# A gated attention and long-convolution kernel: spectrum and conv rows loaded by GpSimd's queue, four small loads by ScalarE's, and both order strings replaced

## The chip, the cores and the metric

The kernel runs on one core of a Trainium2 chip. Its time is the device time of one execution in microseconds (us). TensorE (PE) does the matmuls, VectorE (DVE) and ScalarE (ACT) the elementwise work, GpSimd (POOL) and SyncE (SP) mostly issue DMAs; ScalarE can issue them as well. [...]

## The reference

Eight batches of 3136 rows. First a gated attention with a squared relu in place of a softmax, then a gated long convolution over the sequence, done with a Fourier transform, and an output projection:

```python
# u, v: (8, 3136, 256); z: (8, 3136, 64)
scores = (1 / 3136) * z @ z.transpose(0, 2, 1)
x = u * (np.maximum(scores, 0.0) ** 2 @ v)
proj = x @ w_proj                       # (8, 3136, 768)
x1, x2, x3 = proj[..., :256], proj[..., 256:512], proj[..., 512:]
X2 = np.fft.rfft(x2, n=3136, axis=1)
H = np.fft.rfft(filter_fft, n=3136, axis=0)[None]
x2_conv = np.fft.irfft(X2 * H, n=3136, axis=1)
out = (x1 * x2_conv * x3) @ w_out       # float32
```

## The kernel before, in words

**Tiles.** The sequence of a batch is cut into seven chunks (five of 512 columns, one of 256, one of 320) and 25 tiles of 128 rows. A score block is `ps_s <- zT_t`; its relu goes to `R_t`, its square to `A_t`, and `ps_o_t <- A_t,v_t` adds it up. The scores are symmetric, so some blocks aren't computed again: SyncE transposes an `A_t` by DMA into `M_t`, `M2e_t` or `M2o_t` (line 1848), and TensorE uses these in a later chunk.

**After a chunk.** VectorE multiplies the sum with `uT_t` into `xT_t`. Projections of `xT_t` give the gates (`gate_t`) and `x_t`. `dft1` multiplies `x_t` with a 64-point transform, the result is evicted to `s_t`, and SyncE puts it into a DRAM scratch, `spec` (line 1007).

**After a batch.** 3136 = 64 x 49. `add_spectrum` loads rows of the scratch in the other order, four loads of 16 frequencies' rows each into `spec_in_t` (two buffers), multiplies with 49-point transforms `S`, then with the filter's spectrum `H` on VectorE, transforms back (`xh` with `TZ`) and puts `gs_t` into a second scratch (line 1358). `load_spec` (line 1037) issues three DMAs for each load; it waits for the puts of the batch's chunks, for a free buffer, and for the load before it. `add_end` loads that second scratch chunk by chunk into `conv_in_t` (two buffers, `load_c`, line 1064), transforms (`T`), multiplies with the gates into `yT_t`, projects with `wo` and stores `ost_t` to `out_dram` (line 1467). This work is spread over the next batch's attention as filling work. The filter's own spectrum goes through `load_spec` as well, once.

**The last batch** has nothing behind it. There `load_parts` (line 1052) splits each of the four spectrum loads: a first piece of the transforms' rows that are there early, and a small second piece of 9 rows (two DMAs each) that waits for the last puts. The first two loads go to `spec_in_t`, the other two to `gs_t`. The last conv loads go to `A_t` and `v_t`.

**GpSimd** issues the loads of u, v and z that cast to bf16 (`cast_u`, `load_rows`, `cast_rows`), each group behind a `tick`, a small copy that waits for a chunk's `xT_t` (line 643). u and z are then transposed by DMA from SyncE (lines 1521, 1575).

**What sets the order.** All work is first described as tasks. `Plan.go` plays them through with costs and due times of its own and emits them in the order that results. Two strings, found by a search outside the kernel, make its choices: each letter of `ORDER` says which queue TensorE takes its next task from (S scores, Q quads of the spectrum, W sums over v, w and v such a sum in two row halves, A and B projections, transforms and ends, Z the same late in the last batch), and each letter of `ENGINES` gives one free eviction or square to ScalarE or VectorE. S, Q, w and v run in 64-row parts of the array, the others over 128 rows. SyncE and GpSimd get their DMAs in the order in which the plan finds them ready. `LATE_...` values are allowances that the plan adds to a DMA's landing; `MOST` says how many single PSUM banks it may hold at once.

Of the kernel before, what the change touches and what calls it, by code (L numbers as in the profile page):

```python
# [38 lines left out]
MOST = 3  # L39
# [7 lines left out]
    "ASSAWSSSWWAAWSwvwSvSSwvwSSvWSSSWBWWSSWWWWWSSSWWWWWAwwSSSvWvSSSWWWWWAWWWAWBASBWWWWAASwSwSvwvSSBWAAWAW"  # L47
    "SSSvWWWAWABWAWABWAWWBBAWWSSSWWSSWWSSSWAAWWWSSSWWAWBWABWAAWWWWSSwwSSvBWBAWSvSSWWWWWWAWWWAASSWWABWWAWB"
    "WAASwSSvSWBAWAAWSSWWBWWAAWWAWWSSwSWAAAWSwSSWAAWvSSvSWWAWWWWAWSSAWWAAWWSSSWAWWWAASSwQvwSSAAWASvQSWWWW"
    "AWAWWSQSWWWAAAWSwQSvwSwQSvvwSQSWWWAASSvAWWWWAAWSSQWWWWSSAAWAWQwSSvwSwSQvvwSvSQWWAWWWSQQWWAAAWWWWSwSQ"  # L50
    "WWAAAWQSSwSWvSSvWAWAWWAAWQQSWAWAWWQSSWWAWWSQSWAASSWWAAWQQQWWAWWWSQWWAAWSSWAAWAWWWwSwQSvSvWWSQSWWWSSA"
    "WAWWWWSwSSwwSvSSvvWWAAAWWWSSSWWWWAAWAWAWWWSSwSvSBBAWWBBAWSSAAWSwSSWABBWAWASSvWWABBWWBWSSWWWBABWABAWS"
    "SSWAAWWSSSWBWASSBWAWWWBAWWWBAAWWBAAWBWSSAAWSSABWAAWSSSWWBBAWSQQWWWWWBWQSAWWWWSwSwwQvQvSvSWABWBASQAWB"
    "WQSQWAWAAWBWWSSQWWAAWWSSWAWSSQWAWSQQWSwwQSvvSAWWAWWAWWWSQQWWAWAWWSSSWWWBWAAAQSWAWWWSSSWWWSSAWAWWSSSW"
    "AAWSwSvSWWAWWAWWWAWWSSSWWWWBWSSSWAAWBBWSAAWSSSWWBBWBWSSBBWBAWWAWWBAWWASSWABAWSwSSWABAWBSSBAWBWSSvSWW"
    "BBWWWAABWAAWWSSSWWAWAWQSAABWWQSSWWWBAWSSAWAWBAWQSSWWWWSQSWWABWWAWQSQWWQSQWWBASSWWAAAWWQSAWWAWSQBAWWA"
    "WSSSWWBWSQQWWQSSWWAWWSSSWWWAWWQSWWAWWWAAWASwSAWWSSvQWAWWQSSWWAAWWSSAWAAAWAWSSSWBAAWWSSSWWWBSSWAWWWWW"
    "BWBBWWBAWASSwwSSWAAWBAWSSSvvwSABWBABWBASvSWBWBWWBWAAWWBWSSSWWBAAWAABSSWBwSSSWWBWBAWSvSSWABAWWAWWSSWA"
    "BWWABWSSSWBWSQAAWWAASSWWQQSWAWAWWBAAQQWWBWWBSSWWWWSSQWWWSQSWAAAWSSSWWAAWWWQQSWWBWAAWAWWQSSwQWSQWWSQS"
    "WWWAWWQQvSWAWWAWAWAWWWWAASSWWAWSSSWWQSAAWWWSSSWWAAWAAWAWSSWWAwSwSSvvwSvSWWWAWWAWWWSSBWWBWASSWAAWSSSW"  # L60
    "ABWWBSSAWAWBWASAWBAAWBWWBWAWSSSWWBBSSWWAWBWABASwSvSSWBABWBWSSSWWWABWBWWWSSWBWWWSSSWWAAWSSSWWSQSWAAWA"
    "SSAWAWABWAWABWAWAWWBWAWQQwSSWvSSQWWBWQQSWAWAWWAWSQSWWWWQSQWWBAWSSBWWSSQWWAWWSwSQvSWWABWAWWWAQSWBAWWA"
    "ASQWAWWQSAAWWSSSWWAAWAWWWSSSWWWAWwSSwQvvQSSWWAAWSSWWABWBWWWWWAAWSSSWWWAAWSSSWABWWSSSWABWBAWABBSSWAWA"
    "WWBBAWAWBSSWBBWAWBSSAWAWBASSWAAWSSSWBBBWAWSSSWBWAAWWSSWBBWWAAWAWAWAWSSSWWWAWSwQSvwQSvWWWABWAAAWWWQQS"
    "WWWAASSWBAWSSWBWBAAASSWSQQWWWSSQWWBWBAWWAWWQSSWAWBWAAAWQQQWWSSQWWWSQSWAWAAWWQQSWWAWAWSSWWWAWAAWQWAWS"
    "SSWWAWWSSABAWWSSSWWWWwSSSWWABAWWvSSSWWAAWSSWBWAWWWBWAWASSWBBAWWSSSWAASSWABWWBAWSSSWWWBSSBBWWWAWAWBWB"
    "AWBABWSSWBBAWWSSSWBBWSwSSvSWWWWBBAWWBBWWSSQWWBSSQWWWBAWWSQSWWSSSWAAWWWWWQQWWSSWWAAWWSSQWWQSSWWAAWWAA"
    "WSSQWWWBWWQSSWAWAWWSQQWWQSSWWWSSSWWAWAWWWWWQSSWWWWBAAWWQQSWABAWSSWAWWQSBWWWSSSWWWWWAWWSSSWWWWZWWWWWW"
    "ZAZAZZAAZBAZBZZBZBBZBZZBZBQQZZZQQQQQZZBBQQQQQQQBQQZZZBZZZZBZZZBZBZZZBZZZZZZBBBBBBBBBBBBBBBBBBBBBBBBB"
# [146 lines left out]
class Task:  # L216


    def __init__(self, emit, cost, deps=(), takes=(), prio=0, lat=None, moves=0.0, late=0.0):
        self.emit, self.cost, self.takes, self.prio = emit, cost, list(takes), prio  # L220
        self.lat, self.moves, self.late = lat, moves, late
        self.deps = [d if isinstance(d, tuple) else (d, None) for d in deps]
        self.kids, self.frees = [], []
        self.left = len(self.deps)
        self.ready = 0.0
        self.end = None
        self.holders = 1
        self.ports = ()
        self.second, self.split, self.flips, self.flip = None, False, False, None
        for d, _ in self.deps:  # L230
            d.kids.append(self)
# [9 lines left out]
class Plan:  # L241


    def __init__(self):
# [11 lines left out]
        self.bus = 0.0  # L256
        self.port = {"DVE": 0.0, "POOL": 0.0}
# [32 lines left out]
    def run(self, task, engine, start):  # L290
# [4 lines left out]
        if engine == "PE" and start < SLOW_TO:  # L295
            cost *= 2
        end = start + cost
# [133 lines left out]
def kernel(  # L431
# [599 lines left out]
    def load_spec(src, j0, nj, deps, late=0.0, home=l_p):  # L1031
        box = {}

        def go():
            box["t"] = home.tile([P, 8, D], BF16)
            for rows, part in by_row(src, box["t"], 2 * j0, 2 * nj):
                nc.sync.dma_start(out=part, in_=rows)

        t = on("SP", go, 1.5, [*deps, *((d, ISSUED) for d in loads[-1:])], [home.slots], moves=0.345 * nj, late=late)
# [4 lines left out]
    def load_parts(src, j0, nj, first, rest, home):  # L1044
        box = {}

        def go(lo, hi):
# [3 lines left out]
            for r in range(2):  # L1051
                nc.sync.dma_start(out=box["t"][r * N1 + lo : r * N1 + hi, 0 : 2 * nj, :], in_=rows[r])

        a = on("SP", lambda: go(0, LATE_Q), 1.0, first, [home.slots], moves=0.29 * nj, late=1.0)
        return a, on("SP", lambda: go(LATE_Q, N2), 1.0, [*first, *rest, (a, ISSUED)], prio=-1, moves=0.06 * nj, late=0.5), box

    def load_c(src, c, deps, home):
# [3 lines left out]
        def go():  # L1061
            box["t"] = home.tile([P, 4, D], BF16)
            view = src[ds(t0 * P, nt * P), :].rearrange("(t p) d -> p t d", t=nt)
            nc.sync.dma_start(out=box["t"][:, 0:nt, :], in_=view)
# [3 lines left out]
        return on("SP", go, 0.55, deps, [home.slots], moves=0.235 * nt, late=1.7), box  # L1068
# [113 lines left out]
    def add_proj(b, c, xt, xt_tasks):  # L1182
# [49 lines left out]
        def to_spectrum():  # L1232
            t0, n = T0[c], len(tiles[c])
            at = 0
            while at < n:
# [13 lines left out]
                def ev2(e, nt=nt, box=box):  # L1249
# [9 lines left out]
                        [e2, t1_done], (a, 1), late=LATE_PUT * (b < B - 1),  # L1259
# [248 lines left out]
    plan.bus = 17.5  # L1508
# [8 lines left out]
    def load_uT(b, c, deps):  # L1517
# [9 lines left out]
        if isinstance(made, tuple):  # L1527
            t = after(on("SP", go, 1.3, deps, [uT_p.slots], moves=0.385 * u_tiles(c), late=LATE_TURN), made[1])
            t.frees.append((Held(un_p.slots, made[0]), 0))
        else:  # L1530
            t = on("SP", go, 1.3, [*deps, made], [uT_p.slots], moves=0.385 * u_tiles(c), late=LATE_TURN)
            t.frees.append((made, 0))
        u_tasks[b, c] = t
# [17 lines left out]
    def casts_at(b, c):  # L1551
# [3 lines left out]
        if n < B and 0 <= i < 4:  # L1555
            t0, t1 = ((0, 8), (8, 16), (16, 22), (22, NT))[i]

            def go_z(tick_):
# [26 lines left out]
                t = on("SP", turn, 1.3, [d, *z_tasks.get(n, [])[-1:]], [zT_p.slots] if first else [], moves=0.196 * (t1 - t0), late=LATE_TURN)  # L1585
                t.frees.append((d, 0))
# [233 lines left out]
    def mirror(un, q_):  # L1820
# [13 lines left out]
        for a, i, ts in runs:  # L1834
# [18 lines left out]
            )  # L1853
            made.append(t_)
# [212 lines left out]
```

## Time and profile before

| | |
|---|---|
| runs | 971.87 us median of 3 (966.74 to 972.98) |
| profiled execution | 974.7 us, span 972.9 us, granted TensorE clock 0.992 |
| TensorE busy | 939.0 us (97%) |
| VectorE, ScalarE busy | 862.1 us (89%), 839.6 us (86%) |
| GpSimd busy | 198.0 us (20%) |
| DMA moved | 170.36 MB, 64.6% of the DMA engines' span by SyncE's queue, 23.8% by GpSimd's |

A row of a stretch has its start and end, its length, and for TensorE, its weight loads, VectorE, ScalarE and GpSimd the busy time with the count of instructions, then the granted TensorE clock, the DMA engines' busy share and GB/s. A row of the chain has start, length and what it was; the chain is followed back from the last instruction to what released each step. `SPq` and `ACTq` are instructions of an engine's sequencer, DMA issues above all. A row of a line has a count, then shortest, median and longest duration in ns, first and last start.

### The profile page before, as it was taken

How to read it: one execution, taken by the hardware profiler on the slowest of the kernel's cores; microseconds unless marked ns; L12 is line 12 of the kernel's file. 1: busy time of each engine (PE TensorE's matmuls, PEld its weight loads, DVE VectorE, ACT ScalarE, POOL GpSimd, SP SyncE). 2: the span in 40 equal slices, each digit the busy share in tenths (PEclk: the TensorE clock that was granted, in tenths of full speed). 3: DMA queues.
4: the chain of work that ended last, by engine and by line, in shares of the span. 5: the costliest groups of instructions: out<-in, count | busy, mean ns of one | idle time of the engine just before them, and what ended most of it. 6: DMA issues, size and time to landing. Idle time of an engine off the chain costs nothing.

```text
span 972.9 us, 20144 instructions
## 1 busy us (share of the span) xinstructions
PE 939.0 (97%) x7077; PEld 478.1 (49%) x7180; DVE 862.1 (89%) x1499; ACT 839.6 (86%) x1154; POOL 198.0 (20%) x426
## 2 busy tenths in 40 slices
PE   8999999999999999999999999899999999999986
PEld 3344544455444654445544555345554455544644
DVE  8997989998699998999889987689989999998786
ACT  7887899999899889988888998799897999899873
POOL 5223212220311221122111221121212211001031
PEclk9999999999999999999999999999999999999998
DMA  9998989967999889978899798987799968996768
GB/s 154 167 193 162 158 151 180 181 131 138 182 220 196 147 171 191 220 151 161 180 199 191 132 169 160 199 176 144 160 192 212 196 140 174 186 202 109 206 172 252
DMA packets 332406, 170.36 MB, mean 175 GB/s; under 512 B 242598, under 2 KB 307942, under 8 KB 332304
## 3 DMA queue, kind: packets, MB, share of 16 engines
q1 hardware_dynamic: 302496, 132.43, 64.6%
q0 software_dynamic: 29168, 35.13, 23.8%
q10 hardware_dynamic: 640, 1.51, 0.5%
q8 instruction: 56, 0.92, 0.4%
q14 instruction: 46, 0.38, 0.1%
HBM read 90.26 MB, written 53.35 MB: 148 GB/s over the span
## 4 chain that ended last, share of the span: by engine, by line
PE 87%; DMA 5%; DVE 2%; issue 2%; ACT 1%; SPq 1%; DVEq 0%; ACTq 0%
PE ps_o_t L560 46%; PE ps_s L560 35%; PE ps_o_t L1719 6%; DMA M_t<-spec_in_t 1%; DMA M2o_t<-A_t 1%; DMA spec_in_t<-spec 1%; DMA conv_in_t<-spec 1%; DMA ost_t<-in_z_dram 1%; ACT R_t L1918 1%; DVE gate_t L1218 1%; DMA gs_t<-spec 1%; DMA spec<-s_t 0%; SPq L670 0%; DVE x_t L597 0%; DVE yT_t L1407 0%
## 5 line engine op out<-in xcount | busy, mean ns | idle before, releaser
L560 PE MATMUL ps_o_t<-A_t,v_t 128*128 128x512 bf16 (+2 forms) x1768 | 409.8, 355 | 7.1 <-issue 4.6
L1918 ACT ACTIVATE R_t<-ps_s 128x1024 f32<-128x1024 f32 (+3 forms) x347 | 320.8, 957 | 42.9 <-PE ps_s L560 38.9
L560 PEld LDWEIGHTS <-v_t 128*128 128x128 bf16 x2462 | 222.9, 98 | 227.1 <-issue 62.1
L1927 ACT ACTIVATE A_t<-R_t 128x1024 bf16<-128x1024 f32 (+3 forms) x321 | 312.2, 1000 | 7.3 <-DVE R_t L1920 2.7
L1920 DVE TENSOR_SCALAR R_t<-ps_s 128x1024 f32<-128x1024 f32 (+4 forms) x165 | 185.6, 1135 | 27.4 <-PE ps_s L560 20.2
L1929 DVE TENSOR_TENSOR A_t<-R_t 128x1024 bf16<-128x1024 f32 (+2 forms) x171 | 187.7, 1108 | 12.2 <-ACT R_t L1918 11.5
L560 PE MATMUL ps_s<-zT_t 64*128 64x512 bf16 (+5 forms) x1381 | 163.6, 356 | 1.2 <-DVE zT_t L597 0.5
L643 POOL COPY tick<-xT_t 1x1 bf16<-1x1 bf16 x54 | 11.6, 214 | 666.3 <-DVE xT_t L1973 666.3
L560 PE MATMUL ps_s<-xT_t,wp 128*128 128x512 bf16 (+2 forms) x407 | 107.9, 352 | 0.8 <-issue 0.3
L593 ACT ACTIVATE x_t<-ps_s 128x512 bf16<-128x512 f32 (+2 forms) x144 | 80.8, 570 | 30.6 <-PE ps_s L560 26.9
L560 PEld LDWEIGHTS <-zT_t 64*128 64x128 bf16 (+1 forms) x1414 | 53.5, 99 | 83.9 <-issue 63.2
L1310 DVE TENSOR_TENSOR xh<-xh,H 128x1024 bf16<-128x1024 bf16 x120 | 82.0, 685 | 2.9 <-ACT xh L593 1.5
L1973 DVE SCALAR_TENSOR_TENSOR xT_t<-ps_o_t,uT_t 128x256 bf16<-128x256 f32 (+2 forms) x224 | 76.1, 382 | 7.7 <-PE ps_o_t L560 5.9
L1218 DVE TENSOR_TENSOR gate_t<-ps_s,x_t 128x256 bf16<-128x256 f32 (+2 forms) x210 | 71.4, 384 | 10.8 <-PE ps_s L560 8.3
L560 PE MATMUL ps_o_t<-M_t,v_t 128*128 128x512 bf16 (+2 forms) x316 | 71.9, 350 | 0.9 <-DMA M_t<-spec_in_t 0.7
L1407 DVE TENSOR_TENSOR yT_t<-ps_s,gate_t 128x512 bf16<-128x512 f32 (+2 forms) x97 | 58.6, 617 | 9.2 <-PE ps_s L560 6.5
L593 ACT ACTIVATE s_t<-ps_s 128x512 bf16<-128x512 f32 (+1 forms) x83 | 48.5, 590 | 15.8 <-PE ps_s L560 15.0
L634 POOL DMA_DIRECT2D un_t<-in_u_dram x112 | 59.8, 556 | 6.8 <-issue 3.4
L560 PEld LDWEIGHTS <-wp 128*128 128x128 bf16 x448 | 41.6, 98 | 39.2 <-issue 7.6
L653 POOL DMA_DIRECT2D v_t<-in_v_dram x112 | 59.0, 547 | 9.2 <-issue 7.4
L560 PE MATMUL ps_s<-wp,xT_t 128*128 128x256 bf16 x396 | 58.9, 274 | 0.1
L560 PE MATMUL ps_s<-wo,yT_t 128*128 128x256 bf16 (+1 forms) x342 | 52.1, 275 | 0.2
(175 smaller groups left out, 995.2 us busy)
## 6 DMA issues: line engine op xcount, KB each, us to landing
out_dram<-ost_t SPq DMA_DIRECT2D x60, 256.0 KB
spec<-s_t SPq DMA_DIRECT2D x96, 128.0 KB
spec_in_t<-spec SPq DMA_DIRECT2D x56, 192.0 KB
spec<-gs_t SPq DMA_DIRECT2D x56, 192.0 KB
v_t<-in_v_dram POOLq DMA_DIRECT2D x80, 128.0 KB, 4.7
un_t<-in_u_dram POOLq DMA_DIRECT2D x80, 128.0 KB, 5.3
conv_in_t<-spec SPq DMA_DIRECT2D x34, 256.0 KB
out_dram<-ost_t SPq DMA_DIRECT2D x18, 128.0 KB
```

The costliest lines, as they stand in the source:

```text
L560: wrote(nc.tensor.matmul(o, *args, **kw), o)
L593: got = nc.scalar.activation(out_, in_, AF.Copy)
L634: nc.gpsimd.dma_start(out=t[ds(j * N1, N1), lo - t0 : hi - t0, :], in_=x[:, n2 : n2 + hi - lo, :])
L653: nc.gpsimd.dma_start(out=t[ds(j * N1, N1), ds(v_at(a), (b - a) * D)], in_=r[:, n2 + a - lo : n2 + b - lo, :].rearrange("p t d -> p (t d)"),)
L1218: got = nc.vector.tensor_tensor(g[:, ::-1] if h == 0 else g, p, x, ALU.mult)
L1310: nc.vector.tensor_tensor(x[:, 1 - i], x[:, 0], h, ALU.mult)
L1407: got = nc.vector.tensor_tensor(yb["y"][:, dh, 0:w], p, gates[b, c, dh][:, 0:w], ALU.mult)
L1918: has_read(nc.scalar.activation(r, p, AF.Relu), p)
L1920: has_read(nc.vector.tensor_single_scalar(r, p, 0.0, ALU.max), p)
L1927: nc.scalar.activation(a, r, AF.Square)
L1929: (nc.vector if e == "DVE" else nc.gpsimd).tensor_tensor(a, r, r, ALU.mult)
L1973: nc.vector.scalar_tensor_tensor(x, f, inv_s2, ut, ALU.mult, ALU.mult)
```

## The change

- `load_spec` issues on GpSimd's queue in place of SyncE's, and so does `load_c` where it fills `conv_in_t`.
- In `load_parts` the small second pieces for `gs_t` go to ScalarE's queue; those for `spec_in_t` and all first pieces stay on SyncE's.
- The plan gets new allowances, and a term `CLOGS`: a transposing DMA costs it more while loads from GpSimd or an earlier transpose are still under way. `MOST` goes from 3 to 6.
- `ORDER` and `ENGINES` are other strings of the same lengths and, for `ORDER`, the same count of each letter. `ENGINES` has 15 letters more for VectorE.

The strings are left out:

```diff
-LATE_PUT, LATE_LOAD, LATE_TURN, LATE_C, LATE_D2 = 1.0, 1.8, 1.0, 1.0, 1.6
-LATE_CAST = 1.5
-LATE_Z = 4.0
+LATE_PUT, LATE_LOAD, LATE_TURN, LATE_C, LATE_D2 = 1.0, 1.8, 0.7, 1.0, 0.5
+LATE_CAST = 1.3
+LATE_Z = 2.2
+CLOGS = ((0.0, 0.0, 0.2, 0.3), (0.0, 0.1, 0.7, 1.2))
-LATE_F = 6.0
+LATE_F = 2.0
-MOST = 3
+MOST = 6
...
+        if task.clogs:
+            cost += CLOGS[self.turned_to > start][min(sum(x > start for x in self.casts), 3)]
...
+            if engine == "POOL":
+                self.casts = [*self.casts[-3:], self.bus]
+            elif task.clogs:
+                self.turned_to = self.bus
...
             for rows, part in by_row(src, box["t"], 2 * j0, 2 * nj):
-                nc.sync.dma_start(out=part, in_=rows)
+                nc.gpsimd.dma_start(out=part, in_=rows)
-        t = on("SP", go, 1.5, [*deps, *((d, ISSUED) for d in loads[-1:])], [home.slots], moves=0.345 * nj, late=late)
+        t = on("POOL", go, 1.6, [*deps, *((d, ISSUED) for d in loads[-1:])], [home.slots], moves=0.345 * nj, late=late)
...
-        def go(lo, hi):
+        def go(lo, hi, by=nc.sync):
...
-                nc.sync.dma_start(out=box["t"][r * N1 + lo : r * N1 + hi, 0 : 2 * nj, :], in_=rows[r])
+                by.dma_start(out=box["t"][r * N1 + lo : r * N1 + hi, 0 : 2 * nj, :], in_=rows[r])
-        a = on("SP", lambda: go(0, LATE_Q), 1.0, first, [home.slots], moves=0.29 * nj, late=1.0)
-        return a, on("SP", lambda: go(LATE_Q, N2), 1.0, [*first, *rest, (a, ISSUED)], prio=-1, moves=0.06 * nj, late=0.5), box
+        a = on("SP", lambda: go(0, LATE_Q), 1.0, first, [home.slots], moves=0.29 * nj, late=1.5 if home is l_p else 2.6)
+        if home is gs_p:
+            return a, on("ACT", lambda: go(LATE_Q, N2, nc.scalar), 1.1, [*first, *rest, (a, ISSUED)], prio=-1, moves=0.06 * nj, late=2.0), box
+        return a, on("SP", lambda: go(LATE_Q, N2), 1.0, [*first, *rest, (a, ISSUED)], prio=-1, moves=0.06 * nj, late=1.5 if home is l_p else 2.6), box
...
-            nc.sync.dma_start(out=box["t"][:, 0:nt, :], in_=view)
+            (nc.gpsimd if home is c_p else nc.sync).dma_start(out=box["t"][:, 0:nt, :], in_=view)
         if home is c_p:
-            return in_order(on("SP", go, 0.55, [*deps, *((d, ISSUED) for d in loads[-1:])], [home.slots], moves=0.235 * nt, late=LATE_C)), box
+            return in_order(on("POOL", go, 0.6, [*deps, *((d, ISSUED) for d in loads[-1:])], [home.slots], moves=0.235 * nt, late=LATE_C)), box
...
-    plan.bus = 17.5
+    plan.bus = 21.0
```

In the built order 142 loads have gone from SyncE to GpSimd (96 for spectra, 46 of conv rows) and four small ones to ScalarE; all other DMAs have kept their engine.

More of the change, by code (lines that the diff above doesn't have):

```diff
@@ L256, in __init__ @@
         self.bus = 0.0
+        self.casts, self.turned_to = [], 0.0
         self.port = {"DVE": 0.0, "POOL": 0.0}
@@ L1063, in go @@
             view = src[ds(t0 * P, nt * P), :].rearrange("(t p) d -> p t d", t=nt)
[L1064 removed]
+            (nc.gpsimd if home is c_p else nc.sync).dma_start(out=box["t"][:, 0:nt, :], in_=view)
         if home is c_p:
[L1067 to L1068 removed]
+            return in_order(on("POOL", go, 0.6, [*deps, *((d, ISSUED) for d in loads[-1:])], [home.slots], moves=0.235 * nt, late=LATE_C)), box
+        return on("SP", go, 0.55, deps, [home.slots], moves=0.235 * nt, late=0.2 if home is A_p else 2.6), box
     def sides(x):
@@ L1258, in to_spectrum @@
                         "FA", lambda box=box, nt=nt: box["x"][:, 0 : nt * D], t0 + at, nt, D1[b % 2],
-                        [e2, t1_done], (a, 1), late=LATE_PUT * (b < B - 1),
+                        [e2, t1_done], (a, 1), late=LATE_PUT if b < B - 1 else (0.2 if c < NC - 2 else 1.7),
                     )
@@ L1527, in load_uT @@
         if isinstance(made, tuple):
-            t = after(on("SP", go, 1.3, deps, [uT_p.slots], moves=0.385 * u_tiles(c), late=LATE_TURN), made[1])
+            t = after(on("SP", go, 1.3, deps, [uT_p.slots], moves=0.385 * u_tiles(c), late=1.0), made[1])
             t.frees.append((Held(un_p.slots, made[0]), 0))
         else:
-            t = on("SP", go, 1.3, [*deps, made], [uT_p.slots], moves=0.385 * u_tiles(c), late=LATE_TURN)
+            t = on("SP", go, 1.3, [*deps, made], [uT_p.slots], moves=0.385 * u_tiles(c), late=1.0)
             t.frees.append((made, 0))
+        t.clogs = True
         u_tasks[b, c] = t
```

85 lines of the change are left out of this document (44 added, 41 removed).

## The prediction

> **What bounds the kernel now.** I read the page first (busy shares, slices), then the busy time in stretches of 25 us, then the chain of waits in order of time, then fine stretches and the timelines of TensorE, SyncE and GpSimd where TensorE pauses.
>
> ```profile
> span 972.9 us, 20144 instructions
> PE 939.0 (97%) x7077; PEld 478.1 (49%) x7180; DVE 862.1 (89%) x1499; ACT 839.6 (86%) x1154; POOL 198.0 (20%) x426
> 800.00:825.00 25.00, 24.89 (x181) 13.21 (x183) 23.29 (x40) 22.87 (x31) 5.02 (x11) 1.00 0.82 168
> 500.00:525.00 25.00, 22.91 (x161) 10.60 (x162) 22.35 (x40) 19.61 (x28) 2.58 (x6) 1.00 1.10 204
> 600.00:625.00 25.00, 21.58 (x141) 9.66 (x139) 18.67 (x26) 20.98 (x24) 3.80 (x8) 1.00 1.12 195
> 625.00:650.00 25.00, 24.73 (x166) 11.60 (x166) 20.00 (x39) 20.80 (x28) 3.81 (x8) 0.93 0.86 174
> 925.00:950.00 25.00, 20.26 (x237) 11.24 (x236) 21.09 (x38) 16.95 (x33) 8.66 (x17) 0.93 0.64 178
> ```
>
> TensorE (first pair of figures after the length) is busy in nearly all of an ordinary stretch, 24.89 of 25 us. So the time is TensorE's own work plus a few pauses. Apart from the start and the end, two stretches stand out, 500 to 525 and 600 to 625, and the second is followed by a lower granted clock (0.93). The chain says what ended those pauses, and the fine stretches size them:
>
> ```profile
> 498.26 9.81 DMA M2o_t<-A_t
> 506.00:510.20 4.20, 2.38 (x16) 0.85 (x17) 2.91 (x7) 1.97 (x2) 0.00 (x0) 1.00 1.12 287
> 613.72 1.27 SPq L1037
> 615.03 9.42 DMA spec_in_t<-spec
> 620.00:624.00 4.00, 1.39 (x10) 0.35 (x8) 2.19 (x2) 2.39 (x3) 0.00 (x0) 1.00 1.34 219
> 624.00:628.00 4.00, 3.35 (x19) 1.78 (x20) 2.95 (x5) 1.53 (x3) 0.00 (x0) 0.74 0.84 179
> 628.00:632.00 4.00, 4.00 (x18) 1.35 (x16) 1.51 (x4) 2.39 (x5) 0.00 (x0) 0.83 0.93 199
> 920.38 4.11 DMA spec<-s_t
> 926.71 5.20 DMA gs_t<-spec
> 924.00:928.00 4.00, 2.55 (x31) 1.59 (x29) 2.33 (x6) 1.88 (x4) 2.11 (x4) 1.00 0.60 169
> 928.00:932.00 4.00, 2.02 (x22) 0.96 (x24) 4.00 (x8) 3.65 (x8) 0.00 (x0) 1.00 0.73 240
> 932.00:936.00 4.00, 4.00 (x46) 3.00 (x50) 1.80 (x4) 3.16 (x7) 0.00 (x0) 0.64 0.03 8
> 936.00:940.00 4.00, 3.79 (x62) 1.90 (x59) 4.00 (x8) 3.54 (x8) 3.18 (x6) 0.93 0.63 139
> ```
>
> Three pauses follow. **At 506**, 4.20 - 2.38 = 1.8 us: an `A_t` buffer is free only when a transposing DMA of 9.81 us has read it. **At 620**, (4.00 - 1.39) + (4.00 - 3.35) = 3.3 us: a spectrum load of 9.42 us is late; then the clock falls to 0.74 and 0.83 for two stretches, (0.26 + 0.17) x 4 = 1.7 us of work; 5.0 us in all. **At 924**, 1.45 + 1.98 = 3.4 us: the last batch's spectrum waits for its last put (4.11 us), then its small second pieces (5.20 us); the clock then takes (0.36 + 0.07) x 4 = 1.7 us. Together 11.9 us; more than these, the start and the loose end no move of a queue can win.
>
> **The change part by part.**
>
> *Spectrum and conv loads leave SyncE for GpSimd.*
>
> ```profile
> L1037 SPq DMA_DIRECT2D spec_in_t<-spec x84: 302/513/1942, 144.6 to 871.0; - x84
> L1064 SPq DMA_DIRECT2D conv_in_t<-spec x46: 359/497/1355, 215.2 to 928.7; - x46
> L653 POOL DMA_DIRECT2D v_t<-in_v_dram x112: 509/547/667, 2.5 to 802.5; - x112
> POOL tick L643 <- DVE xT_t L1973: 666.3, 54, 21.4
> DMA to landing us min/median/max: 4.9/5.6/7.0
> 613.72 4.25 SPq L1037 DMA_DIRECT2D spec_in_t<-spec  x6
> 613.42 1.08 POOL L653 DMA_DIRECT2D v_t<-in_v_dram  x2
> ```
>
> 84 + 46 issues, and 12 more for the filter's spectrum by the built order, leave SyncE, 142 of about 0.5 us each (some 71 us); on GpSimd each costs 0.55 us, 78 us. GpSimd sits 666 us waiting in its `tick` copies, so the issue time itself costs nothing; without that cover it would be the 78 us. What can cost is the order: GpSimd now waits for the last put of a batch, and behind that wait stand a `tick` and the u, v and z casts of the next chunk. A tick waits 666.3 / 54 = 12.3 us on average, more than the 4.11 us of a put, so I take nothing for it; the other bound is a rival below.
>
> No load of these rows from GpSimd is in the trace. Its nearest landings are the filter loads of 256 KB, 4.9 to 7.0 us (the sixth row), against 9.42 us for the late load on SyncE. At 613.7 that load needed 4.25 us for six issues while GpSimd sent v rows from 613.4 on, so it ran beside them. In the changed order the six issues and those casts are in one queue, loads of the next spectra ahead of that chunk's casts, and SyncE's transposes no longer stand behind loads. Bounds for the two middle pauses, 1.8 + 5.0 = 6.8 us: all of it gone, or all of it kept (the transfers share the same engines: the DMA share is over 1 in those stretches; and the new search also lowers the planner's allowances for late transfers). Between them I take the middle, **-3.4 us**, since the larger pause is the moved load's own and the smaller is a transpose's.
>
> Here a rule speaks against the change: the Trainium skill, DMA: Bandwidth & Descriptors, section "Issuing engines are not separate DMA queues", says that DMAs started from several engines share the same 16 DMA engines and that spreading them saves only issue time. By that rule this term would be 0 and the time that of the second rival. Another, SBUF — State Buffer, section "SBUF: two separate sides", says that VectorE in a two-port mode keeps GpSimd from writing DMA descriptors. In this trace GpSimd's issues take 509 to 667 ns beside a VectorE that is 89% busy, so such waits, if there are any, are small; the sum has no term for them.
>
> *The last spectrum's small pieces go to ScalarE.*
>
> ```profile
> 924.62 1.69 SPq L1052 DMA_DIRECT2D spec_in_t<-spec  x4
> 926.35 2.21 SPq L1052 DMA_DIRECT2D gs_t<-spec  x4
> L1467 ACTq DMA_DIRECT2D out_dram<-gs_t x2: 517/560/604, 961.6 to 965.2; - x2
> L1467 ACTq DMA_DIRECT2D out_dram<-xh x2: 795/1074/1353, 964.2 to 966.3; - x2
> ```
>
> SyncE issued eight pieces in a row; the first pair for `gs_t` was out only at some 927.4. With ScalarE issuing four beside it, the pair is out after two issues of 0.52 to 1.35 us, between 925.7 and 927.3: 0.1 to 1.7 us sooner; I take 1.3 (nearer to the shorter issues). ScalarE holds still until the put lands, with evictions behind it; they are of work that TensorE has done already, and ScalarE had 0.4 to 0.5 us gaps there anyway.
>
> The order of TensorE ahead of that wait changes too. Behind the last `x_t,T` matmul the kernel before has 6 pairs of `xT_t,wp`, 4 fours of `wo` and 5 fours of conv work ahead of the spectrum; the changed one 8, 6 and 8.
>
> ```profile
> 922.98 0.60 PE L560 MATMUL ps_s<-wo,yT_t 128*128 128x256 bf16 x4
> 923.42 0.59 PE L560 MATMUL ps_s<-xT_t,wp 128*128 128x512 bf16 x2
> 923.85 0.39 PE L560 MATMUL ps_o_t<-T,v_t 128*128 128x128 bf16 x4
> 924.08 0.60 PE L560 MATMUL ps_s<-wo,yT_t 128*128 128x256 bf16 x4
> ```
>
> Start to start these are 0.44, 0.43 and 0.23 us: 5.5 us before, 7.9 after, 2.4 us more cover. It comes from stretches behind the spectrum, where VectorE sets the pace (4.00 of 4.00 us from 936 on), so it isn't missed there. That covers the first wait (1.45 us); of the 1.98 us, 1.3 go with the earlier pieces; the lost clock I halve, 0.9. Together **-3.7 us**; bounds 0 and -5.1.
>
> *Both strings.* ORDER changes 456 times between 64-row work (letters S, Q, w, v) and 128-row work before, 436 times after. The price of a change:
>
> ```profile
> 494.81 0.38 PE L560 MATMUL ps_o_t<-A_t,v_t 128*128 128x512 bf16 x1
> 495.12 0.61 PE L560 MATMUL ps_s<-zT_t 64*128 64x512 bf16 x4
> 495.66 0.60 PE L560 MATMUL ps_o_t<-M2e_t,v_t 128*128 128x512 bf16 x2
> 496.10 0.38 PE L560 MATMUL ps_s<-x_t,T 128*128 128x512 bf16 x1
> ```
>
> Two 128-row matmuls take 0.44 us, one ahead of a change 0.31: 0.31 - 0.22 = 0.09; the four half-row ones, two pairs at once, 0.54 against 0.44: 0.10. So 20 x 0.095 = **-1.9 us**, all on TensorE, which nothing hides. ENGINES gives 15 more of the free evictions and squares to VectorE; at 1.1 us each or less (its 1024-wide square in the page: 1108 ns) that is 17 us at most on an engine with 972.9 - 862.1 = 111 us idle: nothing. MOST and the LATE values emit no instruction; they act through the order alone.
>
> ```profile
> L1929 DVE TENSOR_TENSOR A_t<-R_t 128x1024 bf16<-128x1024 f32 (+2 forms) x171 | 187.7, 1108 | 12.2 <-ACT R_t L1918 11.5
> ```
>
> **Sum.** -3.4 - 3.7 - 1.9 = -9.0 us on the profiled execution's own 974.7 us (span 972.9, 1.8 around it): 965.7. That execution stands 2.8 us above the median of the runs, 971.87, so 962.9 in their terms.
>
> **The rivals.**
> 1. *Every pause goes.* 6.8 + 5.1 + 1.9 = -13.8: 958.1. For it: all three pauses end in a DMA of 5.20 to 9.81 us, where the put took 4.11, and two of these DMAs are loads that the change moves or issues sooner. Against it: the 506 pause is a transpose's, which isn't moved.
> 2. *Transfers take as long from any queue* (the first rule above). The middle pauses stay or come back elsewhere, the tail wins its cover alone: -1.9 - 1.45 = -3.4: 968.5. For it: the DMA share over 1 at both pauses. Against it: the load that was late waited in SyncE's queue too, 1.27 us of issue and the six issues' 4.25.
> 3. *GpSimd's line.* A load that waits for a put holds the tick and casts behind it; the u rows then come late, `xT_t` is late by it, and the next spectrum's puts with it. Each time it decides, TensorE pauses as at 620: 5.0 us with its clock. It decides where the wait is longer than a tick's slack: the mean is 12.3 us, but ticks are uneven. With three of the seven spectra hit, +15.0 - 3.4 = +11.6: 983.5; with two, 978.5. Against it: 80% of GpSimd's span is idle.
> 4. *The change does not do what it says*: excluded for the queues, as the built order has all 142 loads on GpSimd and four on ScalarE.
>
> **How the numbers follow.** Forecast 0.38 (its own range 958.5 to 967.5), rival 1 0.25, rival 2 0.20, rival 3 0.17. A measurement of this kernel tells about 1% from no change: 962.2 and 981.6. Faster by over 1% takes nearly all of rival 1 and somewhat under half of the forecast: 0.41. Slower takes rival 3 with three spectra or more: 0.15. The rest is 0.44. The range goes from 954 (every pause and some of the start) to 980 (two spectra held by GpSimd), leaving out 2 in 10, mostly above.
>
> **What the profile after would show.** Right: spectrum and conv loads under POOL with 0.55 us an issue and landings of 5 to 7 us; ticks waiting some 580 us; no wait of TensorE over 2 us for `spec_in_t`, and the clock at 1.00 between 25 and 920 us; the wait for `gs_t` under 1 us. TensorE's busy time near 937 us would show the fewer changes. Wrong: new waits of TensorE for `spec_in_t`, `M_t` or `zT_t` of 2 us and more in several batches; GpSimd's loads landing after 9 us; DVE waiting for `uT_t`.

## The result, and the profile after

| | time, us (median; lowest and highest) | ratio to before, 95% interval |
|---|---|---|
| before | 971.31 (966.74 to 972.98) | 1 |
| after | 984.82 (981.92 to 992.16) | 1.0147 (1.010 to 1.0195) |

The change makes the kernel 1.5% slower; 962.9 us had been forecast, with a range to 980. The profiled execution took 986.95 us. Three lines of its page, then three views of the same execution: the waits (total us, times, longest), the chain (start, length in us, what) and fine stretches (length; then busy us of PE, PEld, DVE, ACT and POOL; granted clock, DMA share, GB/s).

```profile
PE 951.4 (97%) x7182; PEld 480.1 (49%) x7182; DVE 871.7 (88%) x1514; ACT 833.6 (85%) x1139; POOL 283.5 (29%) x568
spec_in_t<-spec POOLq DMA_DIRECT2D x56, 192.0 KB, 5.9
conv_in_t<-spec POOLq DMA_DIRECT2D x34, 256.0 KB, 4.0
```

```profile
POOL tick L652 <- DVE xT_t L1987: 348.2, 47, 15.6
POOL conv_in_t L1075 <- PE ps_s L569: 132.3, 21, 14.0
POOL spec_in_t L1046 <- PE ps_s L569: 82.6, 18, 11.3
ACT A_t L1941 <- DMA M_t<-A_t: 15.0, 7, 3.0
```

```profile
83.74 8.53 DMA M2e_t<-A_t
180.63 7.45 DMA M2e_t<-A_t
635.35 10.10 DMA M_t<-A_t
927.10 7.96 DMA conv_in_t<-spec
```

```profile
90.00:95.00 5.00, 2.67 (x12) 1.13 (x11) 2.43 (x4) 0.72 (x2) 0.00 (x0) 0.96 0.65 88
95.00:99.00 4.00, 4.00 (x20) 1.45 (x19) 2.04 (x4) 2.41 (x5) 0.00 (x0) 0.62 0.72 180
176.00:190.00 14.00, 7.48 (x70) 3.04 (x69) 6.68 (x10) 7.26 (x9) 3.84 (x8) 1.00 1.24 208
190.00:194.00 4.00, 3.82 (x25) 1.50 (x25) 3.62 (x6) 3.89 (x7) 0.00 (x0) 0.57 1.10 261
643.00:648.00 5.00, 2.25 (x14) 1.21 (x13) 3.40 (x8) 2.68 (x5) 2.05 (x5) 0.96 1.19 188
648.00:652.00 4.00, 4.00 (x16) 1.80 (x15) 1.22 (x1) 3.10 (x6) 1.72 (x4) 0.62 1.03 187
500.00:525.00 25.00, 25.00 (x168) 11.70 (x168) 23.20 (x36) 23.52 (x30) 9.24 (x18) 1.00 1.15 230
600.00:625.00 25.00, 25.00 (x161) 12.28 (x160) 22.51 (x36) 20.36 (x24) 4.88 (x10) 1.00 0.91 165
```

The two middle pauses of before are gone: from 500 to 525 and from 600 to 625 TensorE is busy throughout. Three others stand in their place, at 91, 178 and 644, and each ends with a transposing DMA of 7.5 to 10.1 us that holds an `A_t` buffer. Idle time and lost clock together: 2.3 + 1.5 us, 6.5 + 1.7, 2.8 + 1.5, that is 16.3 us (5.00 - 2.67, then (1 - 0.62) x 4, and so on). The two that are gone had cost 6.8 us, so some 9.5 of the 12.3 us between the two profiled executions (986.95 - 974.7) lie here. TensorE's busy time can't be set against that of before: the profile of after holds 105 matmul records more. ScalarE, which waited once for an `A_t` buffer that a transpose still read (2.7 us), now does so seven times for `M_t` alone (15.0 us). GpSimd's `tick` waits fall from 666 to 348 us, far more than the issue time: two new waits fill the line, for buffers that TensorE frees, 132.3 and 82.6 us.

### The profile page after: what moved, and what is told of

The parts are those of the page before. It is cut to its first block, busy times and chain, and to the rows that moved or that the text cites. A ratio compares the mean times of both kernels' runs of the same rounds, so it can differ in the third digit from the quotient of the medians.

```text
span 985.2 us, 20246 instructions
## 1 busy us (share of the span) xinstructions
PE 951.4 (97%) x7182; PEld 480.1 (49%) x7182; DVE 871.7 (88%) x1514; ACT 833.6 (85%) x1139; POOL 283.5 (29%) x568
## 4 chain that ended last, share of the span: by engine, by line
PE 85%; DMA 7%; DVE 4%; ACT 2%; issue 1%; SPq 1%; DVEq 0%; ACTq 0%
PE ps_o_t L569 45%; PE ps_s L569 35%; PE ps_o_t L1732 5%; DMA M_t<-A_t 2%; DMA M2e_t<-A_t 2%; DMA M_t<-spec_in_t 1%; ACT R_t L1932 1%; DMA conv_in_t<-spec 1%; DVE xh L1321 1%; DMA ost_t<-in_z_dram 1%; DMA A_t<-spec 0%; DVE R_t L1934 0%; SPq L679 0%; DVE xh L606 0%; DMA spec_in_t<-spec 0%
## 5 line engine op out<-in xcount | busy, mean ns | idle before, releaser
L569 PE MATMUL ps_o_t<-A_t,v_t 128*128 128x512 bf16 (+2 forms) x1824 | 418.9, 357 | 0.4 <-DVE xT_t L1987 0.4
L1932 ACT ACTIVATE R_t<-ps_s 128x1024 f32<-128x1024 f32 (+2 forms) x338 | 317.6, 974 | 49.5 <-PE ps_s L569 44.8
L1941 ACT ACTIVATE A_t<-R_t 128x1024 bf16<-128x1024 f32 (+4 forms) x315 | 310.3, 1009 | 23.6 <-DMA M_t<-A_t 15.0
L1934 DVE TENSOR_SCALAR R_t<-ps_s 128x1024 f32<-128x1024 f32 (+4 forms) x174 | 190.3, 1104 | 29.1 <-PE ps_s L569 23.3
L1943 DVE TENSOR_TENSOR A_t<-R_t 128x1024 bf16<-128x1024 f32 (+2 forms) x177 | 192.5, 1102 | 18.5 <-ACT R_t L1932 13.0
L569 PE MATMUL ps_s<-xT_t,wp 128*128 128x512 bf16 (+2 forms) x440 | 115.0, 354 | 3.0 <-DVE s_t L606 2.3
L1075 POOL DMA_DIRECT2D conv_in_t<-spec x46 | 35.9, 784 | 181.4 <-PE ps_s L569 132.3
L1987 DVE SCALAR_TENSOR_TENSOR xT_t<-ps_o_t,uT_t 128x256 bf16<-128x256 f32 (+2 forms) x224 | 76.2, 383 | 12.2 <-PE ps_o_t L569 8.9
L1229 DVE TENSOR_TENSOR gate_t<-ps_s,x_t 128x256 bf16<-128x256 f32 (+2 forms) x218 | 74.1, 385 | 12.9 <-PE ps_s L569 11.5
L1046 POOL DMA_DIRECT2D spec_in_t<-spec x84 | 43.6, 527 | 76.8 <-PE ps_s L569 66.0
L602 ACT ACTIVATE s_t<-ps_s 128x512 bf16<-128x512 f32 (+1 forms) x79 | 45.8, 587 | 20.3 <-PE ps_s L569 14.2
```

What stands on the lines that cost most here:

```text
L569: wrote(nc.tensor.matmul(o, *args, **kw), o)
L602: got = nc.scalar.activation(out_, in_, AF.Copy)
L1229: got = nc.vector.tensor_tensor(g[:, ::-1] if h == 0 else g, p, x, ALU.mult)
L1932: has_read(nc.scalar.activation(r, p, AF.Relu), p)
L1934: has_read(nc.vector.tensor_single_scalar(r, p, 0.0, ALU.max), p)
L1941: nc.scalar.activation(a, r, AF.Square)
```

## The experiments

The two first theories on record below are A, the queue: loads on GpSimd's queue run beside the transposing DMAs, these take longer, and `A_t` buffers come free late; and B, the order: the new strings leave no slack. (A third, that SyncE's line stands still with the loads back on it, fell with the first run.) Ratios are to the kernel before on the same chip.

**The new order, all 142 loads back on SyncE.**

```diff
-                nc.gpsimd.dma_start(out=part, in_=rows)
+                nc.sync.dma_start(out=part, in_=rows)
-            (nc.gpsimd if home is c_p else nc.sync).dma_start(out=box["t"][:, 0:nt, :], in_=view)
+            nc.sync.dma_start(out=box["t"][:, 0:nt, :], in_=view)
```

> The new strings and allowances, but all 142 spectrum and conv loads are issued by SyncE again; TensorE, VectorE and ScalarE keep the changed kernel's order instruction for instruction. Theory A (queue: loads on GpSimd's queue run beside the transposing DMAs and slow them, so A_t buffers come free late and M_t comes late): the pauses at 179 to 188 us go, and with them 7 us and a halved clock, so 972 to 976; the pause at 91 us stays, as no load is near it. Theory B (order: the new strings were found with a smaller allowance for a transposing DMA, 0.7 for 1.0, and have no slack, whatever queue the loads are on): 981 to 990, with pauses behind A_t and M_t as before. Theory C (SyncE gets the loads in an order made for GpSimd and stands still in front of puts): over 990.

975.50 us, ratio 1.0017 (0.999 to 1.0045). The loss goes with the queue: 975.50 lies in theory A's range. But the order with ScalarE's pieces wins nothing that can be measured either.

**The old order, the 142 loads on GpSimd** (the same two lines, the other way, in the kernel before).

> The kernel before, strings and allowances and all, with the 142 loads issued by GpSimd and nothing else changed; TensorE's order is the one of before. Theory A (queue): slower than before, 978 to 990, with pauses of 2 us and more behind transposes of 8 us and more in several batches. Theory B (order): within 1% of before, 963 to 975, and the pause at 620 us, whose late load was one of these, is shorter than 3.3 us.

983.85 us, 1.0129 (1.006 to 1.0195). The queue costs as much in an order that was planned for SyncE, so B falls. Its chain, at the two middle pauses of before and at one of three new ones; then stretches at the two, and TensorE's waits for spectrum loads:

```profile
500.91 11.50 DMA M2o_t<-A_t
619.52 9.67 DMA M2o_t<-A_t
849.63 8.50 DMA spec_in_t<-spec
```

```profile
500.00:516.00 16.00, 9.41 (x54) 3.87 (x53) 7.66 (x12) 8.04 (x11) 3.00 (x6) 0.96 1.20 186
620.00:640.00 20.00, 17.68 (x107) 7.93 (x106) 15.64 (x24) 16.37 (x21) 6.52 (x14) 1.00 1.13 205
PE ps_s L560 <- DMA spec_in_t<-spec: 5.4, 4, 1.8
```

The transpose at 500 takes 11.5 us where it took 9.8, and TensorE is idle for 16.00 - 9.41 = 6.6 us there. At 620 the spectrum load is no longer what TensorE waits for, and 5.0 us of idle time and lost clock have become 2.3 us (20.00 - 17.68, at a clock of 1.00), behind a transposing DMA. So one part of the forecast gain is there, and more is lost elsewhere. Theory A had expected pauses behind transposes in several batches; the chain has these two. At the three new places, 278, 385 and 857, late spectrum loads hold TensorE, 1.8 us at most; in total it waits for them 5.4 us in this view, 4.6 us in before.

**ScalarE's small pieces back on SyncE** (`nc.scalar` to `nc.sync` in the last line of `load_parts`, its task to SP).

> The changed kernel with the four small pieces for gs_t issued by SyncE in place of ScalarE. My prediction held that ScalarE's part wins 1.3 us in the wait for gs_t: then 986 to 987 against the changed kernel's 984.8. If the cover that moved ahead of the wait hides it: no difference, 984 to 986.

984.51 us, 1.0105 (1.004 to 1.017), against 1.0147 (1.010 to 1.0195): no difference can be told. The 1.3 us at stake are 0.13%, far inside these intervals, so the time can't decide between the two forecasts. The profile speaks for the second: with the pieces on SyncE TensorE has no wait for `gs_t` either.

This run shows one thing more. Up to its last 60 us it has the instructions and the queues of after, and its profile still has other pauses (first after, then this run, two stretches each, and this run's chain and GpSimd at the second one):

```profile
165.00:200.00 35.00, 28.29 (x242) 13.27 (x233) 25.34 (x45) 25.77 (x36) 7.02 (x15) 0.95 1.01 155
625.00:670.00 45.00, 42.22 (x277) 18.82 (x276) 38.82 (x68) 34.00 (x44) 17.18 (x35) 0.96 1.03 188
165.00:200.00 35.00, 33.88 (x314) 16.23 (x317) 33.07 (x59) 33.28 (x47) 11.69 (x24) 1.00 1.10 188
625.00:670.00 45.00, 34.80 (x222) 15.44 (x224) 31.63 (x55) 30.62 (x39) 10.36 (x22) 0.91 1.06 158
654.70 10.24 DMA M_t<-A_t
654.61 1.56 POOL L1046 DMA_DIRECT2D spec_in_t<-spec  x3 [5.87 <-PE ps_s L569]
```

The pause at 178 is all but gone, and a longer one has come at 660, behind a transpose of 10.24 us that was issued with three spectrum loads beside it. So a pause belongs to one execution: whether a load and a transpose meet is a matter of a few us. What belongs to the kernel is the time over many runs.

**Only the 96 spectrum loads back on SyncE, the 46 conv loads stay on GpSimd** (the first of the two edits above).

> The changed kernel with the 96 DMAs of spectrum loads back on SyncE, the 46 conv loads still on GpSimd. Theory A: the pauses at 179 to 188 us lie beside spectrum loads, so most of what the queue costs goes, 973 to 978. Theory B: 981 to 990, like the changed kernel.

969.09 us, 0.9969 (0.994 to 0.9996), below theory A's range (973 to 978). The spectrum loads carry the loss; the conv loads on GpSimd cost nothing.

**Why the spectrum loads cost.** In the trace of after, around the pause at 178 (first SyncE's and GpSimd's timelines of after, then the same transposes with all loads on SyncE):

```profile
163.58 1.55 POOL L1046 DMA_DIRECT2D spec_in_t<-spec  x3 [0.40 <-PE ps_s L569]
164.58 11.15 SPq L1861 DMA_TRANSPOSE M_t<-A_t  x2
170.35 1.55 POOL L1046 DMA_DIRECT2D spec_in_t<-spec  x3 [5.22 <-PE ps_s L569]
179.51 0.51 POOL L643 DMA_DIRECT2D un_t<-in_u_dram  x1 [1.95 <-DMA spec_in_t<-spec]
```

```profile
165.72 1.31 SPq L1046 DMA_DIRECT2D spec_in_t<-spec  x3
168.49 4.43 SPq L1861 DMA_TRANSPOSE M_t<-A_t  x2
```

With one queue SyncE issues three loads, then two transposes, and is through the transposes in 4.43 us; with two queues six loads stand beside them and SyncE is held 11.15 us. The last row of after shows a second path: a cast waits until an earlier spectrum load has landed. In the trace GpSimd's DMAs signal eight semaphores in turn (111 to 118), and a cast waits on its own one, so the ninth DMA waits for the first. At 644 this path shows:

```profile
626.40 3.13 POOL L1046 DMA_DIRECT2D spec_in_t<-spec  x6
634.06 1.03 POOL L662 DMA_DIRECT2D v_t<-in_v_dram  x2 [1.91 <-DMA spec_in_t<-spec]
637.86 7.22 SPq L1861 DMA_TRANSPOSE M2e_t<-A_t  x2
```

Here the spectrum loads had gone; the casts behind them came late, and fell beside the transposes. Hence two theories: 1, the bytes beside the transposes; 2, GpSimd's line, held by loads that wait.

**The line held, the bytes from SyncE.**

```diff
-                nc.gpsimd.dma_start(out=part, in_=rows)
+                nc.sync.dma_start(out=part, in_=rows)
+            for k in range(3):
+                nc.gpsimd.dma_start(out=box["t"][50 + k : 51 + k, 0, 0:4], in_=src[k : k + 1, 0:4])
```

> Spectrum loads go from SyncE's queue (as in the run with only the spectrum back on SyncE, 969.1 us, ratio 0.997), but GpSimd issues in the place of each batch three DMAs of 8 bytes into rows of the buffer that nothing reads, so that its line waits for the freed buffer and spends its slots as in the changed kernel (984.8 us). Theory 1 (bytes: the spectrum's packets of GpSimd's queue run beside the transposing DMAs and slow these): no loss, 966 to 972. Theory 2 (line: the casts behind the loads on GpSimd come late and fall beside the transposing DMAs): at least half of the loss comes back, 977 to 985.

973.22 us, 0.9993 (0.9957 to 1.0029). GpSimd's line is nearly as full as in after:

```profile
POOL tick L652 <- DVE xT_t L1989: 361.4, 48, 15.0
POOL spec_in_t L1048 <- PE ps_s L569: 61.7, 13, 11.3
```

973.22 lies 1.2 us above theory 1's range and 3.8 below theory 2's. A line that waits for buffers costs 0.2% over the run with only the spectrum on SyncE (0.9993 - 0.9969), which the intervals don't tell from nothing. Theory 2 falls for this kind of hold. The tiny DMAs land after 4.3 us (median; the whole loads take 5.9), so the hold by loads that have not landed is in it only in part.

**A quarter of the bytes, from GpSimd and from SyncE.**

```diff
-            for rows, part in by_row(src, box["t"], 2 * j0, 2 * nj):
+            box["one"] = True
+            for rows, part in by_row(src, box["t"], 2 * j0, 2):
-        return lambda c: t[:, ds(2 * (n + c), 2), :].rearrange("p c d -> p (c d)")
+        return lambda c: t[:, ds(0 if one else 2 * (n + c), 2), :].rearrange("p c d -> p (c d)")
```

> The changed kernel, but each spectrum load by the common helper fetches 2 of its 8 columns of 512 bytes (a quarter of the bytes), and the transform reads these two in place of all eight; as many DMAs, the same waits for buffers. Theory 1 (bytes): three quarters of the loss go, 968 to 974. Theory 2 (line): the waits for freed buffers stay, 978 to 985; where the line is held by loads that have not landed rather than by buffers, 972 to 978.

> The same quarter of the spectrum's bytes, loaded from SyncE's queue: what fewer bytes win by themselves, to be taken off the quarter from GpSimd. Both theories: 963 to 969. Theory 1 has it within 4 us of the quarter from GpSimd, theory 2 at least 8 us below it.

From GpSimd 974.11 us, 1.0004 (0.9966 to 1.0042); from SyncE 966.89 us, 0.9923 (0.9886 to 0.996). With the whole bytes the queue costs 1.0147 - 0.9969 = 1.8%, with a quarter 1.0004 - 0.9923 = 0.8%, with next to none 0.9993 - 0.9969 = 0.2%. The cost falls with the bytes. Each of these differences is uncertain by about half a per cent, so 0.8% can't be told from a quarter of 1.8%. The 7.2 us between the quarters lie between the two forecasts (4 and 8), and 974.11 lies just above theory 1's range, in the one named for a line held by loads that have not landed (972 to 978). In the two profiles the pause at 178 is in neither; from 625 to 670 TensorE is busy for 38.06 us with the quarter on GpSimd and 44.61 on SyncE. So a part that is not the bytes alone may remain.

**Only the conv loads to GpSimd, in the old order.**

> The kernel before, in its own order, with only the 46 conv loads on GpSimd's queue. In the new order this part won 0.5 per cent (975.5 to 969.1). If the win comes from SyncE's shorter line it comes in the old order too: 966 to 969. If it came from one pause of the new order: 970 to 974.

970.50 us, 0.9974 (0.9935 to 1.0013): on the border of both forecasts; not decided. There is a rival for any gain here: the move takes 21,248 packets of 512 bytes off SyncE's queue and adds 2,656 of 4,096 bytes to GpSimd's, the same bytes in an eighth of the packets.

**The disputed cost by itself.** A kernel of its own: at each start VectorE touches all tiles (its last copy there is L113), then the DMAs go; VectorE copies from each turned tile (L117), ScalarE from each loaded one (L120).

```python
for i, m in enumerate(M):                                # two transposes of 128x1024
    nc.sync.dma_start_transpose(out=m[:].rearrange("p (n j) -> p n j", j=P), in_=A[:, ds(1024 * i, 1024)])
by.dma_start(out=x[r * N1 : r * N1 + 48, 0:8, :], in_=rows[r, 0:48])       # r = 0, 1, two tiles
by.dma_start(out=x[48 : 48 + N1 + 1 : N1, 0:8, :], in_=rows[:, 48])        # and its small piece
```

> Computes nothing of the reference; it measures the disputed cost by itself. Three times each, from a common start: two transposing DMAs of 128x1024 from SyncE's queue, alone and with two batches of spectrum loads (six DMAs, 800 KB) ahead of them or behind them on SyncE's queue, or beside them on GpSimd's or on ScalarE's, or with four casting loads of 64x1024 on GpSimd's. Theory 1 (bytes; a line keeps its order, two lines are mixed packet by packet): transposes alone land after 3 to 5 us; with the loads behind them on the same queue after at most 1.5 us more; with the loads beside them from GpSimd or ScalarE after 7 to 10 us, about when the loads land; beside the casts after 6 to 9 us. Rival (the DMA engines are shared however the loads are issued): transposes with loads behind them on SyncE's queue land as late as with the loads beside them, within 1 us.

VectorE's start and its last copy from a turned tile, twice, first transposes with the loads behind them on SyncE, then transposes with the loads beside them on GpSimd (78.47 - 74.41 = 4.1 us, 147.40 - 138.91 = 8.5):

```profile
74.41 0.14 DVE L113 COPY cast<-zero 128x1 bf16<-128x1 bf16 x1
78.47 0.14 DVE L117 COPY tick_turned<-turned 1x1 bf16<-1x1 bf16 x1 [1.12 <-DMA turned<-A]
138.91 0.14 DVE L113 COPY cast<-zero 128x1 bf16<-128x1 bf16 x1
147.40 0.14 DVE L117 COPY tick_turned<-turned 1x1 bf16<-1x1 bf16 x1 [4.02 <-DMA turned<-A]
```

| us from the start, three times each | both turned | all loaded |
|---|---|---|
| transposes alone | 4.5, 4.4, 4.4 | |
| loads alone, SyncE | | 5.6, 4.9, 5.1 |
| loads alone, GpSimd | | 6.1, 5.8, 5.4 |
| transposes, then loads, SyncE | 4.0, 4.1, 4.3 | 7.5, 8.0, 7.6 |
| loads, then transposes, SyncE | 8.0, 7.9, 8.1 | 5.7, 5.5, 5.2 |
| transposes beside loads, GpSimd | 9.0, 8.2, 8.5 | 8.6, 8.6, 8.3 |
| transposes beside loads, ScalarE | 6.9, 9.2, 9.7 | 8.2, 7.9, 8.9 |
| transposes beside casts, GpSimd | 6.5, 10.8, 10.6 | |

In three tries each theory 1 holds, and its rival, that sharing is the same however the loads are issued, falls: loads behind the transposes in one queue leave these at 4.1 us, loads beside them in another make 8.6 (means). Behind the transposes the loads also start later, as SyncE needs 2.6 us to issue the two; the run doesn't part this from the order in the queue. All the work together takes 7.5 to 9.7 us in each case. A second queue does not make the sum shorter or much longer; it gives up who comes first. Casts are worse than forecast in two tries of three (10.8 and 10.6, 6 to 9 expected).

**The due times.** With the spectrum back on SyncE, once more, and the same with the five old due times:

> The changed kernel with the 96 spectrum loads back on SyncE's queue, once more with more rounds: whether it beats the kernel before. From the first measurement (ratio 0.997, 0.994 to 1.000) theory 1 (bytes beside transposes) expects 0.995 to 0.999; if the new order has only moved the pauses, 0.999 to 1.003.

969.32 us, 0.9968 (0.9937 to 0.9999): this version beats after by 1.8% and the kernel before by 0.3%, where both intervals lie only just below 1.

```diff
-LATE_PUT, LATE_LOAD, LATE_TURN, LATE_C, LATE_D2 = 1.0, 1.8, 0.7, 1.0, 0.5
-LATE_CAST = 1.3
-LATE_Z = 2.2
+LATE_PUT, LATE_LOAD, LATE_TURN, LATE_C, LATE_D2 = 1.0, 1.8, 1.0, 1.0, 1.6
+LATE_CAST = 1.5
+LATE_Z = 4.0
-LATE_F = 2.0
+LATE_F = 6.0
```

> The same with the five due times of the kernel before (LATE_TURN 1.0, LATE_D2 1.6, LATE_CAST 1.5, LATE_Z 4.0, LATE_F 6.0) under the new strings: SyncE's transposes, the casts and the filter's loads are placed by other times. If the new due times make the new pause at 91 us (3.1 us idle, and 5 to 7 us behind the kernel before by 110 us), it goes: 962 to 967. If the strings make it, it stays and the times change the rest either way: 967 to 976.

992.58 us, 1.0215 (1.018 to 1.025), beyond the range forecast. The pause at 91 stays (6.00 - 2.05 = 4.0 us), so it comes with these strings under either set of times:

```profile
90.00:96.00 6.00, 2.05 (x11) 0.85 (x9) 2.43 (x4) 0.69 (x2) 0.00 (x0) 0.99 0.77 100
```

These times also change the order that is built on every engine, so the run says that strings and times go together, not which time costs what.

## Why the prediction was wrong, step by step

**What bounds the kernel**: right in kind. TensorE's own work and a few pauses, most of them ended by a DMA, set the time before and after.

**Term 1, the loads leave SyncE (-3.4 us, bounds -6.8 and 0): wrong in sign.** It measures 1.3% in both orders: 1.0129 in the old one, 1.0147 over 1.0017 in the new one, some 12.6 us. The step that failed is the sentence that counted it a gain that SyncE's transposes "no longer stand behind loads", with a bound of "all of it kept". Standing in one queue kept the loads from mixing with the transposes. The sum had no term for a transpose beside a load, and its row was quoted there: the 9.81 us `M2o_t` at 498, issued in the midst of GpSimd's seven casts (below, before; the spectrum loads ahead of it in SyncE's queue had moved by 500). Measured afterwards, two transposes land after 4.4 us alone, after 8.2 to 9.0 beside loads and up to 10.8 beside casts. That difference, 4 to 6 us each time, was the loss bound that was missing. What the term had right is the load itself: at 620 in the old order TensorE no longer waits for it.

```profile
496.70 1.56 POOL L634 DMA_DIRECT2D zn_t<-in_z_dram  x3 [0.42 <-issue]
498.22 1.08 POOL L653 DMA_DIRECT2D v_t<-in_v_dram  x2
499.23 1.09 POOL L634 DMA_DIRECT2D un_t<-in_u_dram  x2
```

The bytes can be followed in the traces. From their DMA packets I counted, in steps of 1 us from 20 to 920 us, the steps with over ten packets of 256 bytes on SyncE's queue (the transposes) and over 20 KB in packets of 4,096 bytes on GpSimd's (spectrum and conv loads, few others):

| kernel | such steps | ratio |
|---|---|---|
| before | 2 | 1 |
| new order, all on SyncE | 5 | 1.0017 |
| conv alone on GpSimd, old order / new order / new order again | 32 / 35 / 40 | 0.9974 / 0.9969 / 0.9968 |
| the same, due times of before | 32 | 1.0215 |
| the line held, bytes from SyncE | 36 | 0.9993 |
| after / with the pieces on SyncE | 86 / 98 | 1.0147 / 1.0105 |
| old order, all on GpSimd | 96 | 1.0129 |

The run with the due times of before loses without such steps, so its loss is another one. In after a transposing step with at most 20 KB of other packets moves 576 packets of 256 bytes on average (243 steps), one beside these loads and at most 20 KB of others 302 (73 steps). The waits go the same way: ScalarE and VectorE wait 12.0 to 27.7 us for an `A_t` that a transpose still reads in the three kernels with whole spectrum loads on GpSimd (after 21.6), 15.7 with the quarter, and 2.7 to 9.7 in all those with them on SyncE (before 2.7).

**Term 2, the tail (-3.7 us): the wait went, the gain did not come from where it was put.** No wait for `gs_t` is left, with or without ScalarE's pieces. The place of that wait is taken by a conv load of 7.96 us from GpSimd at 927, and the clock is still lost once, 0.50 from 948 to 952. The 0.55 us an issue on GpSimd was right for the spectrum, too low for conv:

```profile
L1046 POOL DMA_DIRECT2D spec_in_t<-spec x84: 501/517/587, 147.3 to 876.9; - x84
L1075 POOL DMA_DIRECT2D conv_in_t<-spec x46: 744/784/879, 228.7 to 937.2; - x46
```

**Term 3, the strings (-1.9 us): not seen in the total.** With terms 2 and 3 together -5.6 us were forecast for the new order; on SyncE's queue alone it measures +0.2% (-0.1 to +0.45%). The price itself may be right: TensorE's busy time, named near 937 us as the sign of it, is 937.9 us there and 939.0 in before, with two matmul records' difference. But the new order takes away the pauses at 506 and 620 without any move of a queue, which term 1 had tied to the queue (so that they are gone in after is luck for term 1), and puts in the one at 91:

```profile
92.00:97.00 5.00, 1.96 (x10) 0.82 (x9) 2.23 (x4) 0.32 (x1) 0.00 (x0) 1.00 0.78 164
506.00:514.00 8.00, 7.79 (x57) 3.38 (x57) 7.61 (x11) 7.79 (x11) 1.20 (x3) 1.00 1.19 226
614.00:640.00 26.00, 25.84 (x160) 12.78 (x162) 24.68 (x42) 19.00 (x26) 5.03 (x11) 1.00 0.97 209
```

The failed step is that the order was priced by its changes of row count alone, and its own pauses were not looked for.

**Rival 2 (968.5)** came from the Trainium skill, DMA: Bandwidth & Descriptors, section "Issuing engines are not separate DMA queues": DMAs of all engines share the 16 DMA engines and interleave. The runs agree with that much (the sum of both transfers stays at 7.5 to 9.7 us). Its conclusion, that another issuing engine only saves issue time, they do not bear out: the transposes went from 4.1 to 8.6 us. The same page of the Trainium skill says, in its section "Queues, rings and completion order", that each DMA engine takes turns between queues, a packet at a time (its packet is a group of descriptors, not the packet counted here). The rate that falls by half (576 to 302) is what such turns would give; no run here shows the turns themselves. This is the rule that should have been weighed.

**Rival 3 (983.5)** gave nearly the time that came, by another mechanism: GpSimd's line held by buffers alone costs 0.2%, not told from nothing, and in after TensorE has no wait for `spec_in_t`. Its first step does show, casts held behind the loads (1.91 us at 634), but by loads that had not landed, and what the late casts met were transposes. That its 983.5 us are near 984.82 is luck.

**What was named ahead**: no wait of TensorE for `spec_in_t` over 2 us, median landings of 5.9 and 4.0 us, the `gs_t` wait under 1 us: as said. The landings of 4.9 to 7.0 us stand in the fifth row of the prediction's lines, not the sixth; they are read rightly. Ticks at 580 us (348) and the clock at 1.00 (0.57 to 0.62 behind each pause): not as said. Of the signs of being wrong, GpSimd's loads landing after 9 us did come (up to 12.2 us), and TensorE waited for `M_t` once for 2.5 us and more, not in several batches.

**Still open**: how much of the cost of the bytes comes by loads beside transposes (178) and how much by casts held until loads have landed (644). The runs do not separate these. Nor is it shown what makes the pause at 91, beyond that it comes with the strings and ends in a transpose of 7.1 to 9.1 us that runs beside casts.

## What to carry to other kernels

Before a load is moved to another queue, look for what it kept its distance from: in the runs here what one queue issued first landed first, and a second queue mixed large packets with small ones. Price every transposing DMA on the chain once alone and once beside a load, and give a moved transfer a loss bound of that difference. Move the transfers whose consumers and neighbours are not in the chain (here the conv loads ahead of the tail, which cost nothing that could be measured) and leave the others behind the transposes they must not meet. And don't price a kernel by the pauses of one profile: with the same instructions they came at other places.

## What the runs showed of the hardware that was not expected

- Two transposes of 128x1024 land after 4.4 us alone, 4.1 with six loads (800 KB) behind them in the same queue, 8.6 with these loads beside them from GpSimd, 6.9 to 9.7 from ScalarE and up to 10.8 beside four casting loads.
- Mixing is about as bad from ScalarE's queue (8.6 us on average) as from GpSimd's (8.6).
- A DMA of a conv load (256 KB in runs of 512 bytes) costs GpSimd 784 ns to issue, one of a spectrum load (192 KB in rows of 4,096 bytes) 517 ns. From GpSimd's queue the conv load then moves in packets of 4,096 bytes, from SyncE's in packets of 512.
- The granted clock was 0.57 to 0.62 for the 4 us behind the three pauses of after, 1.5 to 1.7 us each, the same behind a pause of 2.3 us as behind one of 6.5. In the trace's clock records it is halved for 3.41 us each time, and these spells lie on a fixed grid of 3.41 us (81.92, 92.16 and 453.97 us between them are whole numbers of it). What counts is the cell of the grid just ahead. In after the one ahead of 94.6 holds 1.07 us of TensorE's work, and the clock is halved. In the kernel with the spectrum back on SyncE a pause of 2.9 us at 92 falls into two cells with 2.40 and 1.53 us, and the clock stays at 1.00:

```profile
91.20:94.60 3.40, 1.07 (x6) 0.39 (x5) 2.24 (x4) 0.32 (x1) 0.00 (x0) 1.00 0.75 106
94.60:98.00 3.40, 3.40 (x17) 1.17 (x15) 1.67 (x4) 1.81 (x5) 0.00 (x0) 0.50 0.68 173
90.43:93.85 3.42, 2.40 (x12) 0.97 (x10) 0.00 (x0) 0.00 (x0) 0.00 (x0) 1.00 0.90 195
93.85:97.26 3.41, 1.53 (x10) 0.62 (x11) 2.89 (x6) 1.50 (x3) 0.00 (x0) 1.00 0.41 91
```

  In the traces of all the whole kernels, from 25 to 918 us, each of the 14 cells with under 1.4 us of work was followed by a halved one, and of the 19 with 1.4 to 1.9 us three were.
